# A Mamba-2 scan feeding four mixed experts: other places for a table's load, a block's first chunk and the state updates

## The chip, the core and the metric

The kernel runs on one core of one Trainium2 chip. The metric is device time in microseconds (us) of one launch, as the median over repeated runs. The core has five engines that work side by side, each through its own instructions in their order: TensorE (PE; its weight loads are shown as PEld), VectorE (DVE), ScalarE (ACT), GpSimd (POOL) and SyncE (SP), which here only issues loads and stores. They wait for one another through semaphores. Matrix products land in PSUM, in banks that the other engines read.

## What is computed

Four sequences of 768 tokens go through a state-space layer with 8 heads (head width 32, state 16). Its result, 3072 tokens by 256 features, goes through four two-layer experts whose outputs are mixed by normalized probabilities. Cut to its core:

```python
# layer 1: per batch and head, tokens in order; state is (16, 32)
cum = cumsum(log(clip(a, 1e-6, 1)))           # within a chunk
M   = (C @ B.T) * exp(cum_i - cum_j) * causal # scores times decay
y   = M @ x + (C @ state) * exp(cum)
state = exp(sum(log a)) * state + sum_j exp(cum_end - cum_j) * B_j x_j
# layer 2: four experts, D = 256, F = 1024
p = probs / (probs.sum(-1) + 1e-9)
out = sum_e p[:, e] * (relu(y @ w1[e]) @ w2[e])
```

## The kernel before, in words

All numbers are float32. The 3072 tokens are cut into 24 chunks of 128, and four chunks, one from each sequence, make a block of 512 columns. There are six blocks (index k). A block needs the attention of its four chunks, and then eight expert steps (four experts, each with its hidden layer in two halves). Steps are counted through all blocks as n, from 0 to 47; r is n's place in its block.

**Attention of chunk c.** `load_tokens(c)` brings the tile `xb` (x, B and C), `load_decays(c)` the decays `ab`, broadcast to all partitions, and `ah`. `masks` makes `ctm` from C on ScalarE. `scores` puts four products into four PSUM tiles g (two with the tag `att`, the others in the banks X and Y or in accumulators). `decay_part` has three parts: 0 and 1 are a VectorE scan of 512 elements each, which give the decay matrix LT; after part 1 GpSimd fills the state columns of MT; part 2 is a scan of 128 for `dec`, after which GpSimd multiplies `ctm` into `cts`. `masked` multiplies g and LT into MT, four times on VectorE (L366). `outputs` forms the chunk's columns of yT on TensorE (L379 for the carried state, L385 for MT), and ScalarE copies them out. `carry` renews the state on VectorE with a transpose (L402), a multiply-add (L404) and a masked copy M (L409); the outputs of the same sequence in the next block read it. Tile pools hold three buffers of `xb`, `ab` and `ah`, one of LT and two of MT.

**An expert step.** Both layers run as a seven-product scheme on two-by-two blocks of matrices (after Strassen and Winograd) that needs sums of weights and of activations. `fmul(n, i)` is product i of the first layer (L439), into bank X (i = 1, 6, 7, 4) or Y (2, 5, 3), of which there is one each. ScalarE copies X out (`snap`, L446). VectorE adds Y and a copy into z (`total`, L451), applies relu and the gate (`gated`, L461, tile h), and forms four differences T3, T1, T2, T4 (`diff`, L468, tile hT). `smul(n, i)` is product i of the second layer (L523), one step later, into the accumulators. `fmul(n, 5)` starts bank Y anew, so it has to wait until the z of `total(n, 1)` has been read from it; `fmul(n, 1)` starts X, and has to wait for whoever read X last.

The first two steps (PLAIN = 2) go without the scheme: `plain_first(n, b)` (L487) computes half b of the columns into X and Y by eight products, and `plain_second(n, b, d)` (L504) adds its part of the second layer. These products are written out by hand among the attention of the first block. For steps 2 to 9 GpSimd computes the sums of weights when the weights have landed (`sums_of`, L159 to L162, in `sum_w1` and `sum_w2`), and stores the whole set in DRAM (L168, L173); later blocks load it from there. `sums(k)` forms the activations' sums yS (L417 to L420).

**What sets the order.** The program's text: every engine runs its instructions as they stand there. In the loop over n, the dictionary `enter` says in which step of a block which chunk of the next block gets its masks, decays and scores, and `exit` in which step it gets outputs and carry. In the first block they are {2: 0, 3: 1, 5: 2, 6: 3} and {3: 0, 4: 1, 6: 2, 7: 3}; in later ones {0: 0, 2: 1, 4: 2, 6: 3} and {1: 0, 3: 1, 5: 2, 7: 3}. When a block begins (`ending`), the old block's accumulators are combined, on VectorE and GpSimd.

**The start.** `a_q` holds the decays of the first two chunks for a spread over partitions by products (`spread`, L289 and L296); it is filled with zeros first (L179), and then loaded on two queues. ScalarE's queue brings half of `a_q`, the table `a_sb` of all decays, and `pr`, the experts' probabilities, in this order (L182, L185, L188). GpSimd sums `pr` (L232 to L235), clips `a_sb`, copies it to `a_cut`, and SyncE stores both (`store_decays`), so that later chunks can load them. `divide_gates` (L252, L253) and `store_gates` (L259 to L270) make the first gate tile and a table of all gates in DRAM.

Of the kernel before, what the change touches and what calls it, by code (L numbers as in the profile page):

```python
# [8 lines left out]
FP32 = mybir.dt.float32  # L9
# [3 lines left out]
P = 128  # L13
# [4 lines left out]
def kernel(  # L18
# [37 lines left out]
    nc = tc.nc  # L56

    NCH, _, W = xbc.shape
# [5 lines left out]
    CPB = BLK // P  # L64
# [37 lines left out]
    SPREAD, DIRECT = 2, 3  # L102

    def load_tokens(c):
        xb = load.tile([P, W], FP32, tag="xb", name="xb")
        nc.sync.dma_start(out=xb, in_=xbc[real(c)])
        st.setdefault(c, {})["xb"] = xb

    def load_decays(c, queue):
        if c >= SPREAD:  # L110
            ab = load.tile([P, NH * P], FP32, tag="ab", name="ab")
            nc.sync.dma_start(
                out=ab, in_=(a if c < DIRECT else acut_d)[real(c)].rearrange(
                    "h s -> (h s)").partition_broadcast(P))
            st.setdefault(c, {})["ab"] = ab
        if c >= CPB:
            ah = st[c]["ah"] = load.tile([HN, P], FP32, tag="ah", name="ah")
            queue.dma_start(out=ah, in_=ac_d[real(c)].unsqueeze(1).to_broadcast([NH, N, P]))
# [7 lines left out]
    def load_w1(n):  # L126
        e, jj = divmod(n % SPB, JJ)
        t1 = wt1[n] = wts.tile([P, 7, HB], FP32, tag="wt1", name="wt1", bufs=4)
        if n >= SPB + PLAIN:
            nc.sync.dma_start(out=t1, in_=w1_d[n % SPB])  # L130
            return
        for k in range(2):
            nc.sync.dma_start(
                out=t1[:, 2 * k:2 * k + 2],
                in_=w1[e, k * P:k * P + P].rearrange("p (a f) -> p a f", a=2)[
                    :, :, jj * HB:jj * HB + HB])

    def load_w2(n):
        e, jj = divmod(n % SPB, JJ)
        t2 = wt2[n] = wts.tile([P, 7 * HB], FP32, tag="wt2", name="wt2", bufs=4)  # L140
        if n >= SPB + PLAIN:
            nc.sync.dma_start(out=t2, in_=w2_d[n % SPB])
            return
        for i in range(2):
            f = i * FH + jj * HB
            nc.sync.dma_start(
                out=t2[:, i * 2 * HB:(i + 1) * 2 * HB].rearrange("p (j m) -> p j m", j=JJ),
                in_=w2[e, f:f + HB].rearrange("(j p) m -> p j m", p=P))
# [27 lines left out]
    a_sb = const.tile([NCH * NH // 2, 2, P], FP32, name="a_sb")  # L176

    a_q = const.tile([P, SPREAD, NT, P], FP32, name="a_q")
    nc.gpsimd.memset(a_q, 0.0)  # L179

    for t, queue in enumerate((nc.sync, nc.scalar)):
        queue.dma_start(  # L182
            out=a_q.rearrange("(q r) c t s -> q r c (t s)", q=NQ)[:, t],
# [1 line left out]
    nc.scalar.dma_start(  # L185
        out=a_sb, in_=a.rearrange("c h s -> (c h) s").rearrange("(p r) s -> p r s", r=2))
    load_tokens(0)
    nc.scalar.dma_start(out=pr, in_=probs)  # L188
    load_tokens(1)
    load_decays(2, nc.sync)  # L190
    load_w1(0)
# [59 lines left out]
    def divide_gates():  # L251
        nc.vector.reciprocal(total_p, total_p)  # L252
        nc.gpsimd.tensor_mul(pr, pr, total_p.to_broadcast([P, T // P, E]))  # L253
# [48 lines left out]
    def decays(c):  # L302
        for part in range(3):
            decay_part(c, part)
# [37 lines left out]
    def masks(c):  # L342

        s = st[c]
        m = s["ctm"] = att.tile([HN, NT, P], FP32, tag="ctm", name="ctm")
        for t in range(NT):
            nc.scalar.mul(m[:, t], s["xb"][:, OCT:OCT + P], tmask[:, t:t + 1])
# [14 lines left out]
    def masked(c, qs):  # L362
        s = st[c]
        for q in qs:
            h = slice(NT * q, NT * q + NT)
            nc.vector.tensor_mul(s["MT"][:, h, 0:P], s["g"][q], s["LT"][:, h])  # L366
# [98 lines left out]
    def diff(n, o, x, y):  # L465
        h = hid[n]
        h[o] = ffn.tile([P, JJ, HB], FP32, tag="h" + o, name="h" + o)
        nc.vector.tensor_sub(h[o], h[x], h[y])  # L468
# [177 lines left out]
    scores(0, homes)  # L646
    decays(0)
    spread(1)
    divide_gates()
    store_decays()  # L650
    load_w1(1)
    load_w2(0)
    load_decays(3, nc.sync)
    masked(0, range(NQ))
    masks(1)
    scores(1, banks)
    decays(1)
    outputs(0, ps_att, "att")
    store_gates()
    masks(2)  # L660
    load_tokens(3)
    load_w2(1)
    load_gate(0, 1)
    load_w1(2)
# [24 lines left out]
    sum_w1(2)  # L689
    sum_w2(2)  # L690
    plain_second(0, 1, 2)
    plain_second(1, 1, 1)
    plain_second(1, 1, 2)
    sums(0)
    plain_first(0, 2)
    plain_gated(0, 2)
    carry(0)
    carry(1)
    sum_w1(3)
    sum_w2(3)  # L700
    plain_first(1, 2)
    plain_gated(1, 2)
    carry(2)
    carry(3)


    for n in range(PLAIN, NS):
        k, r = divmod(n, SPB)

        enter, exit = ({2: 0, 3: 1, 5: 2, 6: 3}, {3: 0, 4: 1, 6: 2, 7: 3}) if k == 0 else (  # L710
            {0: 0, 2: 1, 4: 2, 6: 3}, {1: 0, 3: 1, 5: 2, 7: 3})
        c_in, c_out = (CPB * (k + 1) + d[r] if r in d and k < NBLK - 1 else None
                       for d in (enter, exit))
        ending = r == 0 and k > 0
        e = r // JJ
        if r % JJ == 0 and n + JJ < NS:
            load_gate(*divmod(n // JJ + 1, E))
        if n + 2 < NS:
            load_w1(n + 2)
            load_w2(n + 2)  # L720
        opened(n)
        total(n, 1, "11")
        gated(n, "11", "z11")
        if c_in is not None:
            masks(c_in)
            decay_part(c_in, 0)
        sum_w1(n + 2)
        if n > PLAIN:
            sum_w2(n + 1)
        if r == 1 and k > 0:  # L730
            turned_out(k - 1)
        if k > 0 and 1 <= r <= CPB:
            leave(k - 1, r - 1)
        smul(n - 1, 1)
        fmul(n, 6)
        snap(n, 6)
        smul(n - 1, 3)
        if ending:
            keep(k - 1, 0)
        if c_out is not None:  # L740
            outputs(c_out, ps_att, "att")
        fmul(n, 5)
        fmul(n, 7)
        snap(n, 7)
        total(n, 7, "22")
        smul(n - 1, 7)
        smul(n - 1, 5)
        if ending:
            keep(k - 1, 1)
        gated(n, "22", "z22")  # L750
        if c_in is not None:
            decay_part(c_in, 1)
        if c_out is not None and c_out + 2 < NCH:
            load_chunk(c_out + 2)
        fmul(n, 3)
        total(n, 6, "12")
        fmul(n, 4)
        gated(n, "21", "X")
        gated(n, "12", "z12")
        if c_in is not None:  # L760
            decay_part(c_in, 2)
        if c_out is not None:
            carry(c_out)
        if r == SPB - 1 and k < NBLK - 1:
            sums(k + 1)
        smul(n - 1, 6)
        smul(n - 1, 2)
        if c_in is not None:
            scores(c_in, ((ps_att, "att"), (ps_att, "att"), (ps_f, "X"), (ps_f, "Y")))
            masked(c_in, (2, 3, 0, 1))  # L770
        diff(n, "T3", "22", "12")
        if ending:
            combine(k - 1, 0)
            combine(k - 1, 1)
        smul(n - 1, 4)
        diff(n, "T1", "12", "11")
        diff(n, "T2", "22", "T1")
        diff(n, "T4", "21", "T2")
        if ending:
            combine(k - 1, 2)  # L780
    finish(NS - 1)


# [43 lines left out]
```

## Time and profile before

| | |
|---|---|
| median of 7 runs | 660.64 us (659.46 to 665.3) |
| the profiled execution's own time | 660.09 us |
| its span, first to last instruction | 658.3 us |
| granted TensorE clock | 1.00 |
| first plain product (L487) | 17.40 us |
| loop begins (step 2) | 40.94 us |
| block 1 begins (step 8) | 127.47 us |
| HBM traffic | 107.12 MB read, 18.07 MB written |

Times inside the profile are microseconds from the start of the span. A line of the timeline has the start, the duration, the engine, the line of the kernel, the operation, the tile written and the tiles read, the shape and the number of merged instructions; in brackets the idle time before it and what ended that. A group's mean can mix instructions that ran alone with such that ran beside another engine. A busy TensorE isn't TensorE at its peak: its instructions are pipelined, and a wait can be hidden in a long one.

### The profile page before, as it was taken

How to read it: one execution, taken by the hardware profiler on the slowest of the kernel's cores; microseconds unless marked ns; L12 is line 12 of the kernel's file. 1: busy time of each engine (PE TensorE's matmuls, PEld its weight loads, DVE VectorE, ACT ScalarE, POOL GpSimd, SP SyncE). 2: the span in 40 equal slices, each digit the busy share in tenths (PEclk: the TensorE clock that was granted, in tenths of full speed). 3: DMA queues.
4: the chain of work that ended last, by engine and by line, in shares of the span. 5: the costliest groups of instructions: out<-in, count | busy, mean ns of one | idle time of the engine just before them, and what ended most of it. 6: DMA issues, size and time to landing. Idle time of an engine off the chain costs nothing.

```text
span 658.3 us, 8926 instructions
## 1 busy us (share of the span) xinstructions
PE 645.9 (98%) x3355; PEld 539.5 (82%) x3355; DVE 490.0 (74%) x812; ACT 115.5 (18%) x247; POOL 115.7 (18%) x161
## 2 busy tenths in 40 slices
PE   7999999999999999999999999999999999999997
PEld 4788877878888888888888888888888888888886
DVE  7659799897686688776878777769767776856655
ACT  2111111121112122111122121112211212111110
POOL 3368577530000002000003000001100000200000
PEclk9999999999999999999999999999999999999999
DMA  6898877936577434757471667554375544275100
GB/s 213 275 335 236 309 248 246 333 149 184 193 229 258 149 147 126 249 195 240 152 255 60 199 208 258 197 183 144 128 247 176 196 159 166 76 245 192 56 1 32
DMA packets 69874, 125.77 MB, mean 191 GB/s; under 512 B 26680, under 2 KB 52168, under 8 KB 69832
## 3 DMA queue, kind: packets, MB, share of 16 engines
q1 hardware_dynamic: 67004, 110.20, 50.8%
q0 software_dynamic: 2304, 14.68, 5.4%
q8 instruction: 26, 0.43, 0.3%
q10 hardware_dynamic: 524, 0.34, 0.2%
q14 instruction: 16, 0.13, 0.0%
HBM read 107.12 MB, written 18.07 MB: 190 GB/s over the span
## 4 chain that ended last, share of the span: by engine, by line
PE 88%; DVE 8%; issue 2%; ACT 1%; DMA 1%; POOL 0%; SPq 0%; DVEq 0%; POOLq 0%
PE acc L523 38%; PE X L439 22%; PE Y L439 18%; DVE hT L468 3%; PE g L356 3%; PE acc L504 2%; PE y L385 2%; DVE MT L366 1%; PE X L487 1%; DVE z L451 1%; PE Y L487 1%; PE y L379 1%; DVE h L461 1%; DMA xb<-in_xbc_dram 1%; PE a L296 1%
## 5 line engine op out<-in xcount | busy, mean ns | idle before, releaser
L451 DVE TENSOR_TENSOR z<-Y,snap 128x512 f32<-128x512 f32 x138 | 94.5, 685 | 123.8 <-ACT snap L446 107.2
L523 PE MATMUL acc<-hT,wt 128*128 128x256 f32 x736 | 183.2, 382 | 0.0
L446 ACT COPY snap<-X 128x512 f32<-128x512 f32 x138 | 80.8, 585 | 470.4 <-PE X L439 468.4
L523 PEld LDWEIGHTS acc<-hT,wt 128*128 128x128 f32 x736 | 138.2, 190 | 24.3 <-issue 6.3
L439 PE MATMUL X<-yS,wt 128*128 128x256 f32 x552 | 141.7, 379 | 0.0
L523 PE MATMUL acc<-h,wt 128*128 128x256 f32 x552 | 141.5, 379 | 0.0
L439 PEld LDWEIGHTS X<-yS,wt 128*128 128x128 f32 x552 | 104.8, 190 | 14.5 <-issue 0.3
L523 PEld LDWEIGHTS acc<-h,wt 128*128 128x128 f32 x552 | 104.9, 190 | 14.3
L461 DVE SCALAR_TENSOR_TENSOR h<-z,gate 128x512 f32<-128x512 f32 x138 | 97.0, 703 | 3.5 <-PE acc L504 0.4
L439 PE MATMUL Y<-yT,wt 128*128 128x256 f32 x368 | 94.5, 379 | 0.0
L439 PEld LDWEIGHTS Y<-yT,wt 128*128 128x128 f32 x368 | 68.7, 189 | 10.9 <-DVE h L461 0.3
L468 DVE TENSOR_TENSOR hT<-h,hT 128x512 f32<-128x512 f32 x92 | 72.5, 788 | 3.2
L468 DVE TENSOR_TENSOR hT<-h,h 128x512 f32<-128x512 f32 x92 | 62.8, 720 | 0.4
L338 POOL TENSOR_TENSOR MT<-xb,LT 128x128 f32<-128x128 f32 x20 | 8.4, 421 | 268.4 <-DVE LT L333 136.4
L333 DVE TENSOR_TENSOR_SCAN LT<-ab,ident 128x512 f32<-128x512 f32 x44 | 55.5, 1265 | 0.1
L439 PE MATMUL Y<-yS,wt 128*128 128x256 f32 x184 | 49.8, 393 | 3.3 <-DVE z L451 3.3
L439 PE MATMUL X<-yT,wt 128*128 128x256 f32 x184 | 47.4, 380 | 0.6 <-DVE MT L366 0.5
L439 PEld LDWEIGHTS Y<-yS,wt 128*128 128x128 f32 x184 | 32.9, 189 | 13.4 <-DVE z L451 6.8
L461 DVE SCALAR_TENSOR_TENSOR h<-X,gate 128x512 f32<-128x512 f32 x50 | 34.3, 687 | 9.9 <-PE X L487 5.4
L366 DVE TENSOR_TENSOR MT<-g,LT 128x256 f32<-128x256 f32 x96 | 33.9, 415 | 10.0 <-PE g L356 9.9
L439 PEld LDWEIGHTS X<-yT,wt 128*128 128x128 f32 x184 | 34.8, 190 | 6.0 <-DVE MT L366 1.4
L316 POOL TENSOR_TENSOR cts<-ctm,dec 128x256 f32<-128x256 f32 x20 | 14.5, 725 | 122.3 <-DVE dec L313 115.4
(95 smaller groups left out, 341.1 us busy)
## 6 DMA issues: line engine op xcount, KB each, us to landing
wt<-w_d SPq DMA_DIRECT2D x76, 896.0 KB, 6.1
w_d<-wt POOLq DMA_DIRECT2D x16, 896.0 KB, 8.0
ab<-acut_d SPq DMA_DIRECT2D x21, 512.0 KB, 6.1
wt<-in_w_dram SPq DMA_DIRECT2D x40, 256.0 KB, 6.3
xb<-in_xbc_dram SPq DMA_DIRECT2D x24, 320.0 KB, 4.2
gate<-p_d SPq DMA_DIRECT2D x23, 256.0 KB, 6.1
out_dram<-ot SPq DMA_DIRECT2D x160, 16.0 KB, 3.4
ah<-ac_d SPq DMA_DIRECT2D x20, 64.0 KB
```

The costliest lines, as they stand in the source:

```text
L316: nc.gpsimd.tensor_mul(cts, s["ctm"], dec.unsqueeze(1).to_broadcast([HN, NT, P]))
L333: nc.vector.tensor_tensor_scan(out=LT[:, i * w:i * w + w], data0=s["a"][i], data1=ident.rearrange("p h s -> p (h s)")[:, :w], initial=0.0, ...
L356: nc.tensor.matmul(out=g.rearrange("p t s -> p (t s)"), lhsT=s["xb"][k, OBT:OBT + P], rhs=s["ctm"][k].rearrange("p t s -> p (t s)"), start ...
L366: nc.vector.tensor_mul(s["MT"][:, h, 0:P], s["g"][q], s["LT"][:, h])
L385: nc.tensor.matmul(out=y[32 * q:32 * q + 32, t, 0:w], lhsT=xb[:, h * D:h * D + D], rhs=MT[:, NT * q + t, 0:w], start=(first and t == 0), s ...
L439: nc.tensor.matmul(out=f[bank][:, j], lhsT=wt1[n][:, w, j * P:j * P + P], rhs=rhs, start=(i in (1, 2, 5) and j == 0), stop=(j == JJ - 1), ...
L446: nc.scalar.copy(out=s, in_=first[n]["X"])
L451: nc.vector.tensor_add(z, first[n]["Y"], first[n][i])
L461: nc.vector.scalar_tensor_tensor(out=h, in0=first[n][src], scalar=0.0, in1=g.unsqueeze(1).to_broadcast([P, JJ, HB]), op0=ALU.max, op1=ALU. ...
L468: nc.vector.tensor_sub(h[o], h[x], h[y])
L487: nc.tensor.matmul(out=f[bank][:, j], lhsT=wt1[n][:, w, j * P:j * P + P], rhs=yT[k][:, i, cols], start=(i == 0 and j == 0), stop=(i == 1), ...
L523: nc.tensor.matmul(out=acc[k, u][:, half], lhsT=w2_op(n, w)[:, j], rhs=rhs[:, j], start=(begins and j == 0), stop=(n % SPB == SPB - 1 and ...
```

## The change

The change touches four things.

1. At the start, `pr` is loaded first on ScalarE's queue. The fill of `a_q` is cut in two: chunk 0's half on GpSimd, chunk 1's on VectorE.
2. `load_tokens` gets four buffers instead of three. `load_tokens(3)` moves up to before `store_decays`, `load_decays(3)` to before `load_w2(0)`, and `divide_gates` to behind `masked(0)`.
3. Chunk 4, the first of the second block, gets its masks and decays behind `sums(0)`, and its scores and masked products among the plain products. `plain_second(1, 1, 1)` and `(1, 1, 2)` move from ahead of `sums(0)` to both sides of them. The carries of chunks 1 to 3 come last. The first block's loop is left with chunks 5, 6 and 7 to enter in steps 2, 4 and 6, and with chunks 4 to 7 to leave in steps 2, 3, 5 and 7.
4. In every loop step, part 2 of the decays (`dec` and `cts`) moves to behind the masked products and T3, and the carry to the end of the step, behind T4 and the last combine.

```diff
-        xb = load.tile([P, W], FP32, tag="xb", name="xb")
+        xb = load.tile([P, W], FP32, tag="xb", name="xb", bufs=4)
...
-    nc.gpsimd.memset(a_q, 0.0)
-
+    nc.gpsimd.memset(a_q[:, 0], 0.0)
+    nc.vector.memset(a_q[:, 1:], 0.0)
+    nc.scalar.dma_start(out=pr, in_=probs)
...
     load_tokens(0)
-    nc.scalar.dma_start(out=pr, in_=probs)
     load_tokens(1)
...
     spread(1)
-    divide_gates()
+    load_tokens(3)
     store_decays()
     load_w1(1)
+    load_decays(3, nc.sync)
     load_w2(0)
-    load_decays(3, nc.sync)
     masked(0, range(NQ))
+    divide_gates()
     masks(1)
...
     masks(2)
-    load_tokens(3)
     load_w2(1)
...
     plain_second(0, 1, 2)
-    plain_second(1, 1, 1)
-    plain_second(1, 1, 2)
     sums(0)
+    masks(4)
+    decays(4)
     plain_first(0, 2)
     plain_gated(0, 2)
     carry(0)
-    carry(1)
     sum_w1(3)
     sum_w2(3)
     plain_first(1, 2)
     plain_gated(1, 2)
-    carry(2)
-    carry(3)
+    plain_second(1, 1, 1)
+    scores(4, ((ps_att, "att"), (ps_att, "att"), (ps_f, "X"), (ps_f, "Y")))
+    masked(4, (2, 3, 0, 1))
+    plain_second(1, 1, 2)
+    for c in range(1, CPB):
+        carry(c)
...
-        enter, exit = ({2: 0, 3: 1, 5: 2, 6: 3}, {3: 0, 4: 1, 6: 2, 7: 3}) if k == 0 else (
+        enter, exit = ({2: 1, 4: 2, 6: 3}, {2: 0, 3: 1, 5: 2, 7: 3}) if k == 0 else (
             {0: 0, 2: 1, 4: 2, 6: 3}, {1: 0, 3: 1, 5: 2, 7: 3})
...
         gated(n, "12", "z12")
-        if c_in is not None:
-            decay_part(c_in, 2)
-        if c_out is not None:
-            carry(c_out)
...
             masked(c_in, (2, 3, 0, 1))
         diff(n, "T3", "22", "12")
+        if c_in is not None:
+            decay_part(c_in, 2)
         if ending:
...
             combine(k - 1, 2)
+        if c_out is not None:
+            carry(c_out)
```

## The prediction

> **What bounds the kernel now.** I read the page first: its busy shares and the engines of the chain of waits.
>
> ```profile
> span 658.3 us, 8926 instructions
> PE 645.9 (98%) x3355; PEld 539.5 (82%) x3355; DVE 490.0 (74%) x812; ACT 115.5 (18%) x247; POOL 115.7 (18%) x161
> PE 88%; DVE 8%; issue 2%; ACT 1%; DMA 1%; POOL 0%; SPq 0%; DVEq 0%; POOLq 0%
> ```
>
> TensorE is the bound nearly everywhere; nothing but its own queue, or a wait of it, can move the time. The 8% of DVE in the chain are the places where it waits. To find them I took the start of every loop step (first product into X) from the timeline, and cut the trace into windows there.
>
> ```profile
> 17.40:40.94 23.54, 23.54 (x140) 19.40 (x137) 13.20 (x25) 1.61 (x6) 12.26 (x18) 1.00 0.89 302
> ...
> 83.63:97.90 14.27, 13.19 (x66) 10.76 (x64) 13.24 (x17) 2.34 (x5) 10.09 (x12) 1.00 0.79 269
> 97.90:113.71 15.81, 14.73 (x85) 11.65 (x83) 15.29 (x22) 2.80 (x7) 11.47 (x14) 1.00 0.74 242
> ...
> 154.57:167.50 12.93, 12.93 (x66) 10.85 (x65) 10.11 (x16) 2.34 (x5) 1.14 (x2) 1.00 0.72 228
> 167.50:180.84 13.34, 13.34 (x76) 11.31 (x74) 8.87 (x18) 2.22 (x5) 0.00 (x0) 1.00 0.66 219
> ```
>
> Columns: window, length, busy time of PE, PEld, DVE, ACT, POOL, granted clock, DMA share, GB/s. The last two are steps without a wait: 12.93 us with a chunk's scores, 13.34 with a chunk's outputs. A step of the last block, with neither, takes 12.09, so scores cost 0.84 and outputs 1.25. Loop steps 2 to 7 (first block) take 14.83, 14.73, 13.13, 14.27, 15.81 and 13.76. Without waits they should take 13.79 (step 2 has four more products of 0.215), 14.18, 13.34, 12.93, 14.18 and 13.34. The difference, 4.77 us, is TensorE waiting. Block 0 has GpSimd summing weights (POOL 10 us a step); later blocks have almost none. What that does is seen at a boundary:
>
> ```profile
> 86.01 2.74 DVE L468 TENSOR_TENSOR hT<-h,hT 128x512 f32<-128x512 f32 x2
> 88.67 0.68 DVE L451 TENSOR_TENSOR z<-Y,snap 128x512 f32<-128x512 f32 x1
> 89.40 1.13 PE L439 MATMUL Y<-yS,wt 128*128 128x256 f32 x4 [1.08 <-DVE z L451]
> ...
> 169.54 1.42 DVE L468 TENSOR_TENSOR hT<-h,hT 128x512 f32<-128x512 f32 x2
> ```
>
> Two subtractions take 2.74 us beside GpSimd and 1.42 without. Over the whole trace 152 of the L468 subtractions had GpSimd idle and took 0.69 on average, and 32 ran beside it and took 1.07. The sum z that follows is then late, and bank Y, which z reads, cannot be restarted.
>
> **Part A, the start.** `pr` goes to the head of ScalarE's DMA queue, and the fill of `a_q` is split over GpSimd and VectorE. Today the first loads of `a_q` are issued at 1.28, after a GpSimd fill of 0.52 that ends at 1.25. Half a fill is 0.26, so SyncE issues `a_q`, and behind it `xb` of chunk 0, some 0.15 earlier; `pr`'s issue (0.45 today) falls into ScalarE's wait for the fill. The first product waits for both halves of `a_q`, and the second for `xb`.
>
> ```profile
> 7.08 0.26 POOL L232 TENSOR_TENSOR pairs<-pr 128x48 f32<-128x48 f32 x1 [3.55 <-DMA pr<-in_probs_dram]
> ```
>
> GpSimd's 3.55 wait for `pr` goes, so the decay tables leave by about 8.0 instead of 9.81 and `ab` of chunk 3 can be requested earlier; but no product waits for these today, so it is worth nothing while TensorE runs from 4.5 to 17.4 in its own order. SyncE's loads are reordered: `xb` of chunk 3 moves ahead of the tables' store (a fourth buffer frees it), `ab` of chunk 3 ahead of the first second-layer weights. That issue has to wait for the table's store (issued 9.81, landed 11.5, so 1.7 later); behind it queue weights needed at 26.5, so this is hidden by over 10 us. Dividing the gates after the masked scores moves 0.28 of VectorE out of their way; covered too. Value -0.15. Ends: -0.5 (the whole fill) and +0.45 (`pr`'s issue not hidden and `a_q` late by it).
>
> **Part B, chunk 4 in the plain products.** `masks` and `decays` of chunk 4 are put after `sums(0)`, and two plain second products (16 passes, 3.46 us) that stood ahead of the second half's first products go behind them.
>
> ```profile
> 29.50 0.43 DVE L417 TENSOR_TENSOR yS<-yT 128x256 f32<-128x256 f32 x1 [2.10 <-ACT yT L391]
> 29.96 0.83 DVE L418 TENSOR_TENSOR yS<-yT,yS 128x256 f32<-128x256 f32 x1
> 30.72 0.94 DVE L419 TENSOR_TENSOR yS<-yT 128x256 f32<-128x256 f32 x1
> 31.58 0.41 DVE L420 TENSOR_TENSOR yS<-yT,yS 128x256 f32<-128x256 f32 x1
> ...
> 36.17 0.69 DVE L461 SCALAR_TENSOR_TENSOR h<-X,gate 128x512 f32<-128x512 f32 x1 [4.17 <-PE X L487]
> ...
> 50.54 1.74 DVE L333 TENSOR_TENSOR_SCAN LT<-ab,ident 128x512 f32<-128x512 f32 x1
> ```
>
> VectorE idles 4.17 us before the gated product h at 36.17; the scans are put into that hole. But the hole was there because of the 3.46 us that move away. `plain_first(0,2)` now starts at 30.57 (34.03 - 3.46) and `plain_first(1,2)` wants bank X at 34.03 (37.48 - 3.46). X is free only when h has read it, and h now stands behind both scans. VectorE: 29.50 + 2.49 for the four sums, two scans, the 128-wide scan `dec`, h of 0.69. With scans at 1.22 (GpSimd idle) and sums at 4 x 0.42 that ends at 34.7; with scans at 1.75 and `dec` at 0.63 at 36.8. So TensorE waits 0.7 to 2.8 where it never waited. GpSimd sums weights from 28.06 to 35.5 today, so I take the sums as measured and one scan of two slowed: 29.50 + 2.49 + 1.75 + 1.22 + 0.42 + 0.69 + 0.03 = 36.1, a wait of 2.0. `ab` of chunk 4 landed at 31.9 today, in time by a hair. The moved pair then covers the masked scores of chunk 4 (1.4), so no second wait follows; the three carries (about 0.8 each beside GpSimd) come later and only have to be done before z at 45.6.
>
> [...]
>
> **Part C, the first block's loop.** Scores of 5, 6, 7 in steps 2, 4, 6; outputs of 4 to 7 in steps 2, 3, 5, 7. The 0.84 of chunk 4's scores leave the loop and are paid in the plain part: zero together. What changes is the waiting. Step 2 now has outputs and a double last product, both cover for VectorE: its wait of 1.04 goes. The wait of 0.52 for masked scores behind a carry (step 6) goes as the carry moves behind. Two kinds of boundary remain. Scores, then outputs in the next step (4 to 5, 6 to 7): Y is wanted 6.29 after the masked scores start (193.16 to 199.45); VectorE needs 4.67 alone and 6.86 beside GpSimd (97.29 to 104.15). The moved `dec` adds 0.42 but holds GpSimd back over one subtraction (-0.38): 6.9, a wait of 0.6. Outputs, then a step without (3 to 4, 5 to 6, 7 to 8): as at 89.40, where the step lost 1.34, if GpSimd sums at that moment. Twelve weight sums of 4.1 us remain for some 85 us, a share of 0.58: 0.78 each. Together 2 x 0.6 + 3 x 0.78 = 3.5, against 4.77 + 0.20 (step 8 now): -1.5. Ends: -5.0 with all free, +0.3 with all collided (2 x 0.6 + 3 x 1.34 = 5.2).
>
> **Part D, later blocks.** `dec` moves behind the masked scores and the first subtraction, the carry to the step's end.
>
> ```profile
> 244.91 0.42 DVE L313 TENSOR_TENSOR_SCAN dec<-ah,zeros 128x128 f32<-128x128 f32 x1
> 245.91 1.42 DVE L366 TENSOR_TENSOR MT<-g,LT 128x256 f32<-128x256 f32 x4 [0.58 <-PE g L356]
> ...
> 251.71 0.68 DVE L451 TENSOR_TENSOR z<-Y,snap 128x512 f32<-128x512 f32 x1
> 252.44 1.13 PE L439 MATMUL Y<-yS,wt 128*128 128x256 f32 x4 [0.17 <-DVE z L451]
> ```
>
> Today `dec` costs nothing: VectorE waits for the scores anyway, 0.58 even after it. Moved, its 0.42 stand between the scores and z. Where a step has no old block to combine, z ends 1.6 before Y is wanted (197.83 against 199.45): hidden. In the first step of blocks 1 to 4 TensorE already waits for z, and all of it shows; `cts` on GpSimd (0.72) moves with it, into the subtractions, up to 0.38 more. Four times 0.45: +1.8. Ends: 4 x 0.05 = +0.2, if the combine on GpSimd slides off one subtraction, and 4 x 0.8 = +3.2. The carry's three instructions only change places with the subtractions ahead of the same z: nothing, and its state is read a block later.
>
> **Sum.** -0.15 + 2.0 - 1.5 + 1.8 = +2.15. The profiled execution took 660.09 for its span of 658.3 (1.8 around it), so 662.2; the median of the runs, 660.64, is 0.55 above, so 662.8. Ends: -5.3 and +6.75.
>
> **Rivals.** First, the sums on GpSimd, which slide later as each waits for `cts`, miss VectorE's subtractions: B at 0.7, C at -5.0, D at 0.2, A as above, together -4.25: 656.4. For it: boundary 3 to 4 was free today, as GpSimd waited 3.85 for a load. Against: `cts` releases the sums straight into the subtractions, and the block holds as many as before. Second, slower: in part B the scans of chunk 4 start when `ab` has landed. Each us beyond 31.9 costs one us. From 32.9, with the scans beside GpSimd (3.5, `dec` 0.63, h 0.69, X free at 37.7, a wait of 3.7), the sum passes +3.3; at 33.5 it is 4.3 in place of 2.0: 665.1. For it: the load queue is at a share of 0.9 to 1.0 there, the last piece landed at 31.88 after an issue at 24.30. Against: the earlier loads of chunk 3 empty that queue sooner. Third, it doesn't do what it says: chunk 4's early scan trades one wait for another and the dec and carry moves vanish in slack: 660.6.
>
> **How the numbers follow.** A measurement of this kernel can tell about 0.5%, 3.3 us, from no change. Forecast 0.39 (662.8), third rival 0.06: within 0.45. Late scans, and collisions that carry parts B and D to their upper ends, 0.37: slower. Free boundaries 0.18: faster. The range leaves out a tenth at each end: 656.8 to 666.8.
>
> **What would show it.** B: a wait of TensorE of some 2 us at L487's third X, put down to VectorE's h. C: step 2 without a wait, steps 4, 6 and 8 begun with waits for z up to 1.3. D: Y's wait in the first step of blocks 1 to 4 grown by about 0.45. A: the first plain product at 17.2. Wrong would be no wait at B, or boundaries all free.

## The result and the profile after

The changed kernel takes 665.5 us (median of 12 runs, 662.94 to 670.61), the kernel before 660.98 beside it (31 runs). The ratio is 1.0067, with a 95% interval of 1.0050 to 1.0085: slower, by a little more than the half per cent that the prediction took as the least that can be told. The profiled execution took 667.67 us for a span of 665.8. It is one of the longer executions: the six runs with a mean granted clock of 0.999 or more have a median of 663.8, the six with 0.994 to 0.997 lie from 665.8 to 670.6. What the clock has to do with it is shown below.

The page of the changed kernel, first its busy shares, then the clock row of its 40 slices and the engines of the chain:

```profile
span 665.8 us, 8912 instructions
...
PE 648.1 (97%) x3355; PEld 541.7 (81%) x3355; DVE 500.3 (75%) x813; ACT 115.5 (17%) x247; POOL 119.2 (18%) x161
...
PEclk9989999989999999999999999999999999999999
...
PE 87%; DVE 8%; DMA 2%; issue 1%; ACT 0%; POOL 0%; SPq 0%; DVEq 0%; POOLq 0%
```

TensorE has as many instructions as before and is busy 2.2 us longer; VectorE is busy 10.3 us longer, with one instruction more. The clock row has an 8 in the third and in the ninth slice (each 16.6 us long), where before all were 9:

```profile
PEclk9999999999999999999999999999999999999999
```

The waits of TensorE by releaser (us in total, times, longest) say where the rest is:

```profile
PE Y L439 <- DVE z L451: 6.8, 7, 2.0
PE X L487 <- DVE h L461: 2.6, 1, 2.6
```

Before, the first group had 3.3 us, and the second did not exist. Cut at the first weight load or product into X of each step, the windows of the changed kernel are (the plain part, then steps 2 and 8):

```profile
17.16:46.11 28.95, 26.30 (x147) 20.75 (x144) 20.70 (x32) 1.85 (x7) 17.62 (x24) 0.94 0.86 303
46.11:61.16 15.05, 15.05 (x88) 12.31 (x86) 10.95 (x20) 2.81 (x7) 4.27 (x7) 1.00 0.57 200
...
127.90:144.78 16.88, 14.88 (x65) 11.97 (x64) 13.40 (x22) 3.52 (x7) 3.27 (x5) 0.90 0.64 226
```

Step 2 has no wait (length equals PE busy). The plain part and step 8 do, and both have a granted clock below 1. All steps, in us (the prediction cut two borders of before 0.11 later, those of steps 4 and 7):

| | loop begins | 2 | 3 | 4 | 5 | 6 | 7 | 8 | 9 | second step (r = 1) of blocks 2 to 4 |
|---|---|---|---|---|---|---|---|---|---|---|
| before | 40.94 | 14.83 | 14.62 | 13.23 | 14.27 | 15.70 | 13.86 | 13.13 | 13.97 | 13.59 |
| after | 46.11 | 15.05 | 13.34 | 13.36 | 13.34 | 13.36 | 13.34 | 16.88 | 14.78 | 14.43 |

So the first block's loop did become nearly free of waits, and more than that was lost on three other stretches. The first is the gated product h in the plain part. The timeline there:

```profile
32.03 3.34 DVE L333 TENSOR_TENSOR_SCAN LT<-ab,ident 128x512 f32<-128x512 f32 x2
35.30 0.88 DVE L313 TENSOR_TENSOR_SCAN dec<-ah,zeros 128x128 f32<-128x128 f32 x1
36.09 0.66 DVE L461 SCALAR_TENSOR_TENSOR h<-X,gate 128x512 f32<-128x512 f32 x1
36.81 3.66 PE L487 MATMUL X<-yT,wt 128*128 128x256 f32 x8 [2.65 <-DVE h L461]
40.30 1.89 PE L487 MATMUL Y<-yT,wt 128*128 128x256 f32 x8
```

The scans begin straight after the sums, with no wait for a load; two take 3.34 (2.44 when alone), `dec` 0.88 (0.42 alone), and h, X and so TensorE are late by 2.65. Then look at the duration of the eight products behind the wait: 3.66, where eight take 1.89 in the next line. The second is the beginning of block 1:

```profile
126.93 0.74 POOL L159 TENSOR_TENSOR wt<-wt 128x256 f32<-128x256 f32 x1
126.95 1.01 DVE L417 TENSOR_TENSOR yS<-yT 128x256 f32<-128x256 f32 x1
...
134.61 1.13 PE L439 MATMUL Y<-yS,wt 128*128 128x256 f32 x4 [2.00 <-DVE z L451]
```

Before, GpSimd had finished its weight sums by then, and the activations' sums ran alone:

```profile
127.23 0.42 DVE L417 TENSOR_TENSOR yS<-yT 128x256 f32<-128x256 f32 x1
127.68 0.42 DVE L418 TENSOR_TENSOR yS<-yT,yS 128x256 f32<-128x256 f32 x1
```

In the changed kernel GpSimd's last set of weight sums begins together with them: all four take 3.73 (1.01, 0.83, 0.94, 0.95) in place of 4 x 0.42, z is 2.00 late, and step 8 is 3.75 longer than before. The third is the first step of each later block, here block 1:

```profile
146.12 0.42 DVE L313 TENSOR_TENSOR_SCAN dec<-ah,zeros 128x128 f32<-128x128 f32 x1
...
146.68 0.72 POOL L316 TENSOR_TENSOR cts<-ctm,dec 128x256 f32<-128x256 f32 x1 [5.71 <-ACT snap L446]
146.77 1.19 DVE L468 TENSOR_TENSOR hT<-h,h 128x512 f32<-128x512 f32 x1
...
151.92 1.13 PE L439 MATMUL Y<-yS,wt 128*128 128x256 f32 x4 [1.37 <-DVE z L451]
```

`dec` stands between the subtractions, and `cts`, which it releases, runs beside the next one: 1.19 instead of 0.68. The wait for z appears in the next step (r = 1), which is 0.8 longer in four blocks.

Why are products slow behind the two long waits? Windows of 3.41 us around the first (same columns as the windows above, the granted clock third from the end):

```profile
33.38:36.80 3.42, 0.79 (x4) 0.36 (x2) 3.42 (x5) 0.00 (x0) 3.23 (x3) 1.00 1.03 415
36.80:40.21 3.41, 3.40 (x8) 2.77 (x9) 2.69 (x3) 0.00 (x0) 3.07 (x5) 0.50 0.76 237
40.21:43.62 3.41, 3.41 (x17) 2.92 (x16) 1.38 (x2) 0.00 (x0) 2.97 (x5) 1.00 0.81 320
```

In the second of them TensorE is granted half its clock, and does 8 products where the next stretch has 17. From 135.78 to 139.20, behind the wait of 2.00 at step 8, it is 0.50 again, with 10 products. What such a stretch costs can be read from the runs below that had the same wait at full clock. In three of their profiles ("`dec` early again", "`dec` late in block 0 only", "all but the split") TensorE waits 2.5 to 2.9 us at this place and is busy for 24.64 in the plain part, against 26.30 here: 1.66 more. Step 8 takes 16.88 here, and 15.18 in "wait filled" with a wait of 1.98 and the clock at 1.00: 1.70 more.

The account of the 7.5 us of span, then: first plain product -0.24; plain part +2.65 (wait), +1.66 (clock) and +0.26 (24.64 busy with a wait, 24.38 in the profiles without one); steps 2 to 7 -3.9 (waits of 0.87 left of 4.77; the 0.84 of chunk 4's scores, which went from here to the plain part, counts as zero together); step 8 +3.75 (1.70 of it the clock); `dec` in four later blocks +3.3. Together 7.5.

### The profile page after: what moved, and what is told of

It reads as the page before. It is cut to its first block, busy times and chain, and to the rows that moved or that the text cites. A ratio compares the mean times of both kernels' runs of the same rounds, so it can differ in the third digit from the quotient of the medians.

```text
span 665.8 us, 8912 instructions
## 1 busy us (share of the span) xinstructions
PE 648.1 (97%) x3355; PEld 541.7 (81%) x3355; DVE 500.3 (75%) x813; ACT 115.5 (17%) x247; POOL 119.2 (18%) x161
## 3 DMA queue, kind: packets, MB, share of 16 engines
q0 software_dynamic: 2304, 14.68, 5.4%
## 4 chain that ended last, share of the span: by engine, by line
PE 87%; DVE 8%; DMA 2%; issue 1%; ACT 0%; POOL 0%; SPq 0%; DVEq 0%; POOLq 0%
PE acc L523 38%; PE X L439 22%; PE Y L439 17%; DVE hT L468 3%; PE g L356 3%; PE acc L504 2%; DMA wt<-in_w_dram 2%; PE y L385 2%; PE X L487 1%; DVE MT L366 1%; PE y L379 1%; PE Y L487 1%; DVE z L451 1%; PE a L296 1%; DMA xb<-in_xbc_dram 1%
## 5 line engine op out<-in xcount | busy, mean ns | idle before, releaser
L468 DVE TENSOR_TENSOR hT<-h,hT 128x512 f32<-128x512 f32 x92 | 76.2, 829 | 3.2
L316 POOL TENSOR_TENSOR cts<-ctm,dec 128x256 f32<-128x256 f32 x20 | 18.8, 940 | 167.6 <-ACT snap L446 163.3
L439 PEld LDWEIGHTS Y<-yS,wt 128*128 128x128 f32 x184 | 32.8, 189 | 17.1 <-DVE z L451 10.2
```

What stands on the lines that cost most here:

```text
L316: nc.gpsimd.tensor_mul(cts, s["ctm"], dec.unsqueeze(1).to_broadcast([HN, NT, P]))
L439: nc.tensor.matmul(out=f[bank][:, j], lhsT=wt1[n][:, w, j * P:j * P + P], rhs=rhs, start=(i in (1, 2, 5) and j == 0), stop=(j == JJ - 1), ...
```

## The experiments

Each was compared with the kernel before on the same chip. The columns are those of the table of steps, from one profiled execution of each kernel; the ratio and its 95% interval are from all its runs (4 to 12) and those of before beside it:

| run | loop begins | 2 | 3 | 4 | 5 | 6 | 7 | 8 | 9 | r = 1 later | ratio to before |
|---|---|---|---|---|---|---|---|---|---|---|---|
| `dec` early again | 43.22 | 15.05 | 13.34 | 16.91 | 13.96 | 13.79 | 13.34 | 13.74 | 13.97 | 13.59 | 0.9995 (0.9974 to 1.0016) |
| scans split | 40.99 | 15.05 | 13.34 | 16.95 | 13.34 | 14.88 | 13.34 | 16.87 | 14.79 | 14.43 | 1.0015 (0.9992 to 1.0038) |
| last sums later | 45.29 | 15.05 | 13.34 | 13.36 | 13.34 | 14.89 | 13.34 | 13.13 | 14.78 | 14.43 | 1.0015 (0.9994 to 1.0036) |
| wait filled | 44.11 | 15.05 | 13.34 | 13.52 | 13.34 | 13.36 | 13.34 | 15.18 | 14.78 | 14.43 | 1.0029 (1.0011 to 1.0047) |
| start only | 39.94 | 13.83 | 16.08 | 13.87 | 14.12 | 15.70 | 13.86 | 13.13 | 13.97 | 13.59 | 0.9986 (0.9973 to 1.0000) |
| `dec` late in block 0 only | 44.12 | 15.05 | 13.34 | 13.37 | 13.34 | 13.52 | 13.34 | 16.88 | 13.97 | 13.59 | 1.0032 (1.0013 to 1.0050) |
| tail behind z | 47.09 | 15.05 | 13.34 | 12.93 | 13.34 | 13.38 | 13.34 | 14.45 | 14.43 | 14.12 | 1.0001 (0.9985 to 1.0016) |
| all together | 40.31 | 15.05 | 13.34 | 13.89 | 13.34 | 13.38 | 13.34 | 12.93 | 13.62 | 13.34 | 0.9884 (0.9865 to 0.9902) |
| before, tail behind z | 40.54 | 14.68 | 14.19 | 13.34 | 14.36 | 14.88 | 13.97 | 12.93 | 13.62 | 13.34 | 0.9935 (0.9920 to 0.9950) |
| all but the split | 43.05 | 15.05 | 13.34 | 13.61 | 13.34 | 13.66 | 13.34 | 12.93 | 13.61 | 13.34 | 0.9946 (0.9927 to 0.9964) |
| all, `dec` early | 41.00 | 15.05 | 13.34 | 13.38 | 13.34 | 14.14 | 14.31 | 12.93 | 13.61 | 13.34 | 0.9904 (0.9890 to 0.9918) |

Two things limit what one profile of each can say. The start varies: the first plain product begins at 15.79 to 17.16 us in the eleven profiles of kernels with the changed start, and at 17.40 and 16.73 in the two with the old one, so "loop begins" carries a microsecond and more of that. And the first block varies: "last sums later" has the changed kernel's code up to step 8, yet step 6 takes 14.89 in its profile and 13.36 in the changed kernel's.

**`dec` early again.** The changed kernel, with part 2 of the decays back ahead of the scores in every block; the carry stays at the step's end.

```diff
         gated(n, "12", "z12")
+        if c_in is not None:
+            decay_part(c_in, 2)
...
         diff(n, "T3", "22", "12")
-        if c_in is not None:
-            decay_part(c_in, 2)
```

> The changed kernel with one part undone: the 128-wide scan dec and the product cts stand ahead of the scores again in every loop step; the carry stays at the end of the step. Theory (dec's 0.42 us, and cts beside a subtraction, push the sum z past the point where bank Y is wanted in the first step of blocks 1 to 4): the second steps of blocks 2 to 4 fall from 14.43 to 13.6 us, block 1's from 14.78 to 14.0; 3.0 to 3.4 us less in all, median 662 to 662.5. Rival (the late carry is what delays z): these steps stay at 14.4 and the median stays at 665 to 666.

Measured 662.28 us. The later r = 1 steps and step 9 went back to exactly 13.59 and 13.97: the loss there is `dec` with its `cts`, and not the carry, which stayed late. Step 8 fell to 13.74, with a wait of 0.54 in place of 2.00. But at step 4 a wait of 2.08 and a half-clock stretch came in, where GpSimd's sums run beside the subtractions and the carry. That the earlier `dec` put them there isn't shown: the next run has the same at step 4 with a late `dec`.

**Scans split.** Chunk 4's two scans are put behind one pair of gated products each, instead of both ahead of them; `sum_w2(3)` goes behind them too.

```diff
     masks(4)
-    decays(4)
     plain_first(0, 2)
     plain_gated(0, 2)
+    decay_part(4, 0)
...
-    sum_w2(3)
     plain_first(1, 2)
     plain_gated(1, 2)
+    decay_part(4, 1)
+    decay_part(4, 2)
+    sum_w2(3)
```

> The changed kernel with chunk 4's scans among the plain products moved: the first half behind the gated products that free banks X and Y, the second half and dec behind the next pair, the last sum of weights behind them. Theory (in the changed kernel the gated product stands behind both scans, so the third plain product waits 2.65 us for bank X, and TensorE then runs some 3 us at half clock, 1.5 us more): the loop begins at 41.0 to 42.2 instead of 46.11, and the median is 4 us lower, 661 to 662. Rival (the chunk's table lands late, and whatever stands behind the scans waits): the wait moves to the scores of chunk 4 and the loop begins no earlier than 44.5, median 664 to 666.

Measured 662.25. The wait at the plain products is gone: the loop begins at 40.99, 5.12 sooner, of which 4.57 lie behind the first plain product (24.38 us from there instead of 28.95). In the profile 3.6 of it came back at step 4 and 1.5 at step 6. But this execution took 667.58, the longest of the twelve, and over all runs the ratio fell from 1.0067 to 1.0015, about 3.4 us, near the 4 expected; and the 14.88 at step 6 is that of "last sums later", which has no split, so it need not come from the split. VectorE's rows ahead of step 4's z, in this execution:

```profile
73.39 0.20 DVE L402 STREAM_TRANSPOSE S<-A 128x32 f32<-128x32 f32 x1
73.62 0.98 DVE L404 SCALAR_TENSOR_TENSOR S<-S,dec 128x32 f32<-128x32 f32 x1
74.63 0.85 DVE L409 TENSOR_TENSOR M<-S,qmask 128x128 f32<-128x128 f32 x1
75.41 0.68 DVE L451 TENSOR_TENSOR z<-Y,snap 128x512 f32<-128x512 f32 x1
```

The carry (L402 to L409) takes 2.02 beside GpSimd and is directly ahead of z. Ahead of step 8, where GpSimd has finished its sums, the changed kernel's carry takes 0.74. Ahead of step 4 it takes 0.95 there; GpSimd had waited 0.53 for weights, and began its next sums behind the carry.

**Last sums later.** `sum_w2(9)` goes from the start of step 8 to its end.

```diff
-        if n > PLAIN:
+        if n > PLAIN and n != SPB:
             sum_w2(n + 1)
...
+        if n == SPB:
+            sum_w2(n + 1)
```

> The changed kernel with one GpSimd job moved: the sums of step 9's second weights are put to the end of step 8 instead of its start, so that they no longer run beside VectorE's four sums of activations at the end of block 0. Theory (that collision makes z late by 2.0 us in step 8, after which TensorE again runs at half clock): step 8 falls from 16.9 to 13.1 to 13.4 us, the median by 2 to 3.5 us, to 662 to 663.5. Rival (the carry, moved behind the subtractions, makes z late): step 8 stays at 16 to 17 and the median at 665 to 666.

Measured 663.57. Step 8 has 13.13 us, as before the change: its loss is GpSimd's late sums; the carry, which still stands ahead of z here, costs at most 0.2 without them (12.93 in "all together", where it is moved).

**Wait filled.** Three products of a constant tile (`turn`) are put ahead of the late plain products, so that TensorE does not idle.

```diff
     sum_w2(3)
+    turn(3)
     plain_first(1, 2)
```

> The changed kernel with three products of ones (128x512, results unused) put into TensorE's wait ahead of the third plain product; nothing else is changed, and the wait for bank X is as long. Theory (the half speed after the wait comes from TensorE's having been idle): the eight products behind it take 1.73 us instead of 3.15, the loop begins at 44.5 to 44.9 instead of 46.11, and the median falls by 0.5 to 1.5 us to 664 to 665 with less spread. Rival (those products are slow for another reason, such as the loads that run then): they stay at 3.1, the loop begins at 46.1 or later, and the median at 665 to 666.5.

Measured 664.22, and no half-clock stretch in the profile. Of the wait 0.24 is left, the eight products behind it take 2.00 us instead of 3.66, and the loop begins 2.0 earlier although work was added. This alone does not show that the idle time halved the clock: with the wait left as it was, "`dec` early again" and "`dec` late in block 0 only" had no half stretch there either and began the loop at 43.22 and 44.12. The count over all traces, in the last section, is what ties the two together. The long wait at step 8 is still there, 1.98, here without a half stretch.

**Start only.** The kernel before with the first two parts of the change.

```diff
-        xb = load.tile([P, W], FP32, tag="xb", name="xb")
+        xb = load.tile([P, W], FP32, tag="xb", name="xb", bufs=4)
...
+    nc.gpsimd.memset(a_q[:, 0], 0.0)
+    nc.vector.memset(a_q[:, 1:], 0.0)
+    nc.scalar.dma_start(out=pr, in_=probs)
```

> The kernel before with parts 1 and 2 of the change alone (the start and the loads); order of the plain products, first block's loop, dec and carry as before. My account of the changed kernel puts these parts at -0.24 us (first plain product at 17.16 instead of 17.40) and the rest of its loss at parts 3 and 4: so the ratio to before is 0.9996 (within 0.2%), the first plain product starts at 17.1 to 17.2, the loop begins at 40.7 and steps 2 to 9 have the lengths of before within 0.3 us. Rival: the moved loads set when GpSimd's weight sums run, and so part of the losses at the boundaries of the first block comes from them: then steps 2 to 9 differ from before by 1 to 4 us in all, with waits for z at other steps, and the ratio leaves 0.998 to 1.002.

Measured 660.27, span 658.2 against 658.3. The total is as expected, the places are not: the first plain product starts at 15.94, not at 17.1 to 17.2, the loop begins 1.00 sooner, step 2 is 1.00 shorter, step 3 1.46 and step 4 0.64 longer. Waits in the first block do lie elsewhere, as the rival said (one profile cannot tell the loads' part in it from the scatter named above), and steps 2 to 8 give back 0.92 of what the start gained. The start is not where the loss is.

**`dec` late in block 0 only.** As the first run, for blocks 1 to 5 alone.

```diff
+        if c_in is not None and k > 0:
+            decay_part(c_in, 2)
...
         diff(n, "T3", "22", "12")
-        if c_in is not None:
+        if c_in is not None and k == 0:
             decay_part(c_in, 2)
```

> The changed kernel, with dec (part 2 of the decays) put back ahead of the scores in blocks 1 to 5 only; in the first block's loop it stays behind T3. My theory: in later blocks the late dec costs 0.85 in each of four steps and brings nothing, so steps r=1 go back to 13.59 (step 9 to 13.97), while steps 2 to 7 keep 15.05, 13.34, 13.36, 13.34, 13.36, 13.34 as in the changed kernel, and step 8 keeps its late z (14.8 to 16.9). Sum -3.4 against the changed kernel: ratio to it 0.995, to before 1.0015. Rival: the order of the later blocks also shifts what the first block's GpSimd does (the step that put dec back everywhere did move step 8); then step 8 falls to 13.1 too and the ratio to before is 0.996 to 0.998.

Measured 663.58. Steps 2 to 7 keep the change's lengths within 0.2, step 8 keeps 16.88, and the later blocks are back at 13.59. With the first run this shows two things: late `dec` in later blocks only costs, and late `dec` in the first block is what sends GpSimd's sums into step 8 (16.88 here and 13.74 there). In the plain part the wait of 2.9 had no half-clock stretch behind it.

**Tail behind z.** The carry and the last part of the combine go from the end of a step to the next step, behind its z and h of half 11.

```diff
         gated(n, "11", "z11")
+        if left is not None:
+            carry(left)
+            left = None
+        if r == 1 and k > 0:
+            combine(k - 1, 2)
...
-        if ending:
-            combine(k - 1, 2)
         if c_out is not None:
-            carry(c_out)
+            left = c_out
```

> The changed kernel, with the carry and the last part of the combine (three VectorE instructions each) moved from the end of a step to the next step, behind its z and h of half 11. Theory: what stands on VectorE ahead of the z of the next step is what TensorE waits for, one for one. So r=1 of blocks 2 to 4 loses the combine's 0.67 (14.43 to 13.76), step 9 its 1.03 (14.78 to 13.75), step 8 the carry's 0.74 and with it perhaps the half clock (16.9 to 14.1 or 15.7); the wait at the plain products stays. Sum -4.2 to -5.8 against the changed kernel: ratio to before 0.998 to 1.001. Rival: the moved instructions are only late elsewhere (they hold up the first scan and the z of half 22, and the outputs of the next step): then the steps after them grow by 0.3 to 0.8 each and the sum is within 1.5 us of the changed kernel, ratio 1.004 to 1.008.

Measured 661.51. Step 8 has a wait of 1.25 instead of 2.00 and no half clock: 14.45. The later r = 1 and step 9 lost 0.3 instead of the 0.67 and 1.03 expected (the later blocks another 0.2 in the step ahead): what stands ahead of z is not worth its whole duration here. The two half-clock stretches of this profile both follow the plain wait of 2.8.

**All together.** Split scans, last sums later, `dec` late in the first block only, tail behind z.

> The changed kernel with everything that the runs so far showed as a loss put right: the scans of chunk 4 split around the gated products, the last second-layer sums of the first block moved to the end of step 8, dec late in the first block only, and the carry and the last part of the combine behind the z of the next step. Additive theory: against the run with split scans alone, step 4 loses the carry's 2.03 and the half clock (16.95 to 13.4), step 6 1.4, step 8 3.7, step 9 1.4, three later r=1 1.1 each: about -13 us from a span of 665.8, so a span of 652 to 654 and a ratio to before of 0.989 to 0.992. Rival: GpSimd's sums only slide to other subtractions, as in the runs that moved one thing (each then had waits of 2 to 4 us in new places): a span of 655 to 658, ratio 0.994 to 0.999.

Measured 654.86 us (653.33 to 654.96): the additive theory holds, with a little more than its range, and this kernel beats both. The gains of the four edits nearly add: alone they took 0.52, 0.52, 0.35 and 0.66% off the changed kernel's ratio, 2.05 in sum, and all at once took 1.83. (The ratio rests on five runs here; that of the medians alone is 0.9905.) Its page, and the windows of the plain part and of steps 4 and 8:

```profile
span 651.5 us, 8925 instructions
...
PE 642.5 (99%) x3355; PEld 539.4 (83%) x3355; DVE 491.4 (75%) x813; ACT 115.5 (18%) x247; POOL 112.7 (17%) x161
```

```profile
17.00:40.31 23.31, 23.31 (x140) 18.67 (x139) 18.06 (x31) 1.51 (x6) 13.95 (x20) 1.00 0.99 337
...
68.70:82.59 13.89, 13.20 (x65) 10.79 (x64) 13.27 (x18) 2.34 (x5) 9.63 (x12) 1.00 0.81 289
122.65:135.58 12.93, 12.93 (x65) 10.85 (x64) 11.49 (x21) 3.52 (x7) 1.13 (x2) 1.00 0.58 230
```

TensorE is busy 99% of the span, waits for z 0.9 us in all (3.3 before; 0.7 of it in step 4) and has no half-clock stretch in any step. The plain part begins at 15.94 here, 1.06 before the first window. From there to the loop, and in step 8, length and busy time are equal: the wait at the start of each block is gone too.

**Before, tail behind z.** The edit of the tail alone, in the kernel before, where the carry stood ahead of the scores.

> The kernel before, with one thing of the best kernel alone: the carry and the last part of the combine stand in the next step, behind its z and h of half 11. None of the change's four parts is in it. My theory: these moves give 0.25 in each r=1 of blocks 2 to 4 (13.59 to 13.34) and 0.6 in step 9, -1.4 in all; in the first block they take the carry out of the way of the masked scores and z, worth 0.5 to 2.0 of the 4.77 us of waits there; the rest needs the change's other order of chunks. Ratio to before 0.994 to 0.997. Rival: the change's order is not needed, the carry alone was what made z late: then steps 2 to 8 come within 1 us of their lengths without a wait and the ratio is 0.990 to 0.992, like the best kernel's 0.9884.

Measured 656.56, ratio 0.9935: a little better than expected, and about half of the best kernel's gain. Steps 5, 6 and 7 keep waits of 1.43, 0.70 and 0.63 (their lengths less 12.93, 14.18 and 13.34). The best kernel is nearly free of waits there, so other edits of it are needed for these; which, the change's order of chunks among them, is not shown.

**All but the split.** The best kernel with the two scans together again, and `sum_w2(3)` back with them.

> The best kernel, with the scans of chunk 4 left together ahead of the gated products, where the change put them (the second-layer sums of step 3 as in the change too). Theory: VectorE's h is late for the third plain product into X by 2.6 to 2.9 us, and nothing later can give that back: the loop begins at 43 to 44.2 instead of 40.31, or at 44.5 to 46 where the clock is halved behind it; steps 2 to 9 as in the best kernel within 0.6. Ratio to before 0.9925 to 0.9965. On the clock: the half-clock stretches seen so far are all 3.41 us long and lie on one grid of that length in each trace; every stretch of the grid in which TensorE stood idle for more than 1.9 us was followed by one, and none with less than 1.7. So a half stretch follows here only if more than half of one stretch of the grid falls into the wait. Rival: the split itself costs the best kernel something in step 4 (13.89 instead of 13.34), so the loss is only 2 us, ratio 0.991 to 0.992.

Measured 657.4, ratio 0.9946: the loop begins 2.74 later (the first plain product starts at 15.94 and 15.95), with a wait of 2.46, and nothing gives it back. No half-clock stretch followed in the profile: the wait lay across a border of the 3.41 us grid, 0.95 and 1.51 on its two sides. Other runs of the same kernel reached 659.89 at lower mean clocks.

**All, `dec` early.** The best kernel with `dec` ahead of the scores everywhere.

> The best kernel, with dec ahead of the scores in the first block too, so that the change's late dec is gone altogether. Theory: with the carry out of the way VectorE has room on both sides of the masked scores, so this moves nothing: ratio to before 0.987 to 0.990, steps 2 to 9 within 0.4 each. Rival: as in the run that put dec back everywhere, it holds up the masked scores and lets GpSimd start its sums 2 us sooner, into the subtractions: waits for z of 0.4 to 2 us come back at steps 4 to 7, ratio 0.991 to 0.994.

Measured 654.63, ratio 0.9904. In the profile steps 6 and 7 are 0.76 and 0.97 longer, as the rival said, and step 4 is 0.51 shorter. Against the best kernel (0.9884, interval to 0.9902) that is no difference which these runs can tell.

## Why the prediction was right and wrong

The time, 665.5, lies in the range, but the forecast itself did not come: 662.8 said less than half a per cent, and the slower case came. Some of that is luck: one half of C came out 1.8 better than forecast and the other 3.2 worse, and the half clock, for which the sum has no term, cost 3.4 in the profiled execution (1.66 and 1.70), which at 667.67 lies above the range. The sum's lower end also has a slip: with B at its 0.7 it is -4.6, not -5.3. By the steps of the prediction, against the profiled execution:

| part | forecast | its ends | measured |
|---|---|---|---|
| A, the start | -0.15 | -0.5 to +0.45 | -0.24 |
| B, wait at the third X | +2.0 | 0.7 to 2.8 | +2.65, and +1.66 of half clock |
| C, steps 2 to 7 | -2.1 (-1.5 less 0.58) | | -3.9 |
| C, step 8 | +0.58 (0.78 - 0.20) | +1.14 at the collided 1.34 | +3.75 |
| D, later blocks | +1.8 | 0.2 to 3.2 | +3.3 |

- **A** was small, as forecast: the start alone measures 0.9986 (0.9973 to 1.0000). Its -0.24 cannot be told from the scatter of the first plain product, which is over 1 us.
- **B** had the right mechanism, place and bounds. The size was off by 0.65: "one scan of two slowed" was the choice, and both were (3.34 for two, against 2.97), with `dec` at 0.88 against 0.42. The second rival's cause, a late table, is false: the scans waited for no load. What failed here is the clock, for which the sum has no term: its rows have waits of TensorE of up to 1.08, at a granted clock of 1.00 (the window from 83.63), a wait of 2.0 was forecast, and what one of that length does to the clock none of these rows could tell. It cost 1.66, and 1.70 more at step 8: in the profiled execution, the waits of 2.65 and 2.00 each had a stretch of 3.41 us at a clock of 0.50 behind them.
- **C** was the best and the worst part. The loop did lose its waits, more of them than forecast, as the sums on GpSimd missed the boundaries there. That the late `cts`, which holds them back, did this is argued: in the two profiles with `dec` early some waits came back (2.08, 0.54 and 0.12 at steps 4 to 6; 1.01 at step 7 of the best kernel). But the sum priced 7 to 8 like the other boundaries at no more than 1.34, from a boundary with only subtractions. This one also has the four activation sums (L417 to L420), which doubled beside GpSimd: 3.73 in place of 1.68, and a half-clock stretch, 1.70, on top. The rows of the four sums were in the prediction, at 0.41 and at 0.94 side by side, and were not carried to the place where the same code runs again.
- **D** was the upper end: some 0.8 a block, not 0.45. The half that was counted as "up to 0.38 more" came every time: in every loop step of the changed kernel that has it, `cts` runs beside the subtraction that follows `dec` (1.19 to 1.22 in place of 0.68 in these four steps).
- **The sum** of parts measured without the clock is about +4.1; the clock made it 7.5 in the profiled execution, and the medians differ by 4.5. That is the second rival's "collisions that carry parts B and D to their upper ends" without its late table, and with the loss at step 8, which it did not name.
- **The first rival**, free boundaries, came true for steps 2 to 7 alone. The third, that nothing happens, is false: every part but the start moved something by over 2 us.

## What to carry to other kernels

When one engine is the bound and another feeds it just in time, list what stands in the feeder's queue ahead of the one instruction that is waited for, and move everything else behind it: here the state update and the output's last combine, six instructions that nobody needed soon, gave 0.65% alone. Work put into a hole of the feeder has to be cut to the size of each hole; two scans together cost 2.7 us that one scan in each of two holes did not. And judge an edit by all its runs, not by one trace: in single profiles 3 to 5 us gained at one place seemed to come back at another, but some of that also differed between executions of the same code, and over all runs the gains of four edits nearly added up (2.05% in sum, 1.83% at once).

## What the runs showed of the hardware

**The clock's grid.** Between the first plain product and the end of TensorE's work, the half-clock stretches of all traces are 3.41 us long (once two in a row, 6.83), and where a trace has more than one, their starts lie on one grid of 3.413 us to within 1 ns (in the changed kernel's they are 98.987 us apart, 29 times 3.4133). Idle time of TensorE in one stretch of that grid, and what the next stretch was granted, over the thirteen traces (before, after and the eleven runs):

| idle in the stretch, us | stretches | next stretch at half clock |
|---|---|---|
| 1.99 to 2.63 | 8 | 8 |
| 1.37 to 1.70 | 10 | 0 |

No stretch with less idle time was followed by one, but for the second of the two in a row. So in these traces the length of a wait does not tell whether a half stretch follows; how much of it falls into one stretch does. The plain part of the changed kernel, unaltered in five of the traces, is the plainest case: behind waits of 2.65, 2.68 and 2.79, with 2.63, 2.11 and 2.16 in one stretch, the clock was halved; behind 2.79 and 2.9, with at most 1.63 and 1.52, it was not. The run with `dec` early again has both, in windows on its grid:

```profile
30.53:33.94 3.41, 2.26 (x11) 1.65 (x9) 3.41 (x3) 0.00 (x0) 3.02 (x4) 1.00 1.06 420
33.94:37.35 3.41, 1.77 (x8) 1.59 (x9) 2.72 (x6) 0.00 (x0) 2.99 (x5) 1.00 1.01 224
...
74.90:78.32 3.42, 1.40 (x7) 0.89 (x5) 3.35 (x5) 0.59 (x1) 2.94 (x5) 1.00 1.01 368
78.32:81.73 3.41, 3.35 (x8) 2.72 (x9) 2.39 (x3) 0.00 (x0) 1.32 (x3) 0.50 0.72 296
```

A wait of 2.79 is cut by a border into 1.15 and 1.63, and the clock stays at 1.00; a wait of 2.08 lies all but whole in one stretch, and the next has 0.50. The grid lies differently from trace to trace (a border at 36.80 in the changed kernel's, and at 78.32 in this one, 12 stretches and 0.56 later), and of the five traces with the same plain part, three have a half stretch behind its wait and two have none. The changed kernel's runs spread by 7.7 us, the best kernel's five by 1.6. Long waits seen in the profile are not the whole of it: the kernel before, whose trace has no wait in the loop above 1.08 and no half stretch, spread by 4.7 beside the best kernel, with six of 29 runs at a mean clock of 0.997 or less. If idle time did that too, its waits have to differ between executions, which no trace here shows. What idle time between 1.70 and 1.99 does is open, and so is why one half stretch, itself with 0.63 of idle, was followed by a second.

**VectorE beside GpSimd.** Several instructions of VectorE that read and write SBUF alone were slowed beside GpSimd's sums: a scan from 1.22 to 1.67 on average of two and `dec` from 0.42 to 0.88 (both at the plain products of the changed kernel), the multiply-add of the carry from 0.25 (at step 8 of the changed kernel) to 0.98 (at step 4 of "scans split"). One that reads PSUM was not: h took 0.66 right behind that `dec`, with GpSimd busy; and the sums z, which read PSUM too, took 0.69 on average alone (104) and 0.67 beside it (34) in the changed kernel.
